# Loading queries and keys in long rows and turning them two tokens at a time: one change to an attention and MLP-mixer kernel on Trainium2

## The chip, the cores and the metric

The kernel runs on one core of one Trainium2 chip. A core has a matrix engine (PE, with its weight loads shown apart as PEld), a vector engine (DVE), a scalar engine (ACT), a third elementwise engine (POOL) and a sequencer that issues transfers (SP). Each runs its own list of instructions in order, and they wait for each other through semaphores. Data comes from the chip's main memory into the on-chip buffer by 16 DMA engines; a transfer is issued from the queue of SP or of ACT. PE writes its products into an accumulator memory of eight banks (`ps` in the code), from which DVE and ACT copy them out.

The metric is device time in microseconds (us): the median over runs of the whole program. Lower is better.

## The reference

Two blocks follow each other, all in 32-bit floats as far as the inputs go. The first is attention with routing: queries and keys are each assigned to one of 16 centroids per head, and a query sees only keys of its own cluster. The second is an MLP mixer over tokens, then over channels.

```python
batch, n_heads, seq, head_dim = (4, 8, 768, 64)      # 16 centroids per head
q_n, k_n, c_n = (each divided by its norm + 1e-06)
q_assign = np.argmax(np.einsum('bhsd,hcd->bhsc', q_n, c_n), axis=-1)
k_assign = np.argmax(np.einsum('bhsd,hcd->bhsc', k_n, c_n), axis=-1)
mask = q_assign[:, :, :, None] == k_assign[:, :, None, :]
scores = np.where(mask, 0.125 * np.matmul(q, k.transpose(0, 1, 3, 2)), -1000000000.0)
attn = softmax(scores)                               # over the keys
x = np.matmul(attn, v)                               # to (4, 768, 512), heads side by side
h = np.maximum(x.transpose(0, 2, 1) @ w_tok1, 0.0) @ w_tok2     # 768 -> 256 -> 768
u = x + h.transpose(0, 2, 1)
out = u + np.maximum(u @ w_ch1, 0.0) @ w_ch2         # 512 -> 1536 -> 512
```

The mixer's weights come as 64-bit floats and are rounded to 32 bits on the chip, in 31 pieces.

## The kernel before

**Pairs of heads.** The 32 heads of the four batches are worked on as 16 pairs, `pair(m)` for m = 0 to 15. For one pair, the scores need keys and queries with the 64 head dimensions of both heads on the 128 partitions, and the tokens along the line: the tile `Ts[m % 3]`, twelve blocks of 128 tokens, six of keys (rows 0 to 5) and six of queries (rows 6 to 11). The inputs lie the other way round, tokens first, so each block has to be transposed.

**Two ways to get there.** From pair 3 on, keys and queries are loaded into `qkr` in rows of 1536 bytes (six tokens of one head), split into 16-bit halves on ACT (`part_qk`, L1054), transposed by DMA, and joined again on ACT (`join_qk`, L1068). The first three pairs take a shorter way: `load_qk` (L915) loads them into `qks[m % 2]`, and `turn_qk` (L1036) transposes them on PE. In that buffer a partition holds six tokens, and for each token the 64 dimensions of head 0 next to those of head 1. To lay them out so, `load_qk` issues four transfers for a pair (keys and queries, each head by itself), in rows of 256 bytes (one token of one head). `turn_qk` takes the 128 values of a token position, both heads, as the input of one transpose (`turn`, L853); four transposes fill one bank of `ps`, and one copy (`copy`, L862) of 128 partitions x 512 moves the bank into `T`. That is twelve transposes and three copies a pair. In the profile all transposes and most matrix products have the line of `mm` (L846), copies on ACT have L865, copies on DVE L867, and transfers L905.

**The start.** `begin()` (L946) loads the centroids, then pair 0 on two queues (head 0 on SP, head 1 on ACT), then pair 1 and the first values on SP. While the loads are on their way PE multiplies the identity matrix by itself twelve times (`keep_busy(BUSY)`), and DVE normalises the centroids (`norm`, up to L997). Then pair 0 is turned, the centroids are turned between its banks and copied into `cbd` on DVE, and ACT loads its table for exponentials once `Ts[0]` is complete (L1007).

**Routing.** `route(m, bank)` (L1079) multiplies keys and queries with the centroids on PE, and DVE finds the largest of each group of 16: transpose (L1098), maximum, comparison, transpose back. For pair 0 the result is written straight into the mask operand `M0` in eight pieces (DVE L1131 and L1136, ACT L1129); for later pairs it goes through main memory (`wdm`). `scores(m)` (L1161) works in twelve chunks over three pairs of banks: two products of keys and queries, two products that add the mask, and one exponential on ACT (L1205) over both heads. For pair 0, three chunks' products are issued ahead, then pair 1 is turned, then the masks follow, and after the third mask the routing of pair 1, `route(1, 6)`. `values` (L1249) multiplies the exponentials with the values; pair 2 is turned between the third and the fourth of pair 0's six groups of value products, and routed after the sixth.

**The order of the work.** All operations are first collected in a `Program`, with the buffers that they read and write, and a cost for each engine that may do them. A planner (L152) then runs a list schedule: PE's operations stay in the order in which they were added, each other engine takes what it can start, the one with the earliest due time first. An operation that may run on ACT or DVE goes to the engine that would finish it first. An `after` gives the earliest planned time of an operation: `START + STEP * n` for the load of weight piece n. The planned order is what each engine's instruction list is written in.

**After the pairs**, DVE rounds what is left of the weight pieces (L1380 to L1390, L885), and the token and channel mixing runs on PE, with sums on DVE and POOL (L885).

## Time and profile before

| | |
|---|---|
| median of three runs | 789.43 us (789.10 to 789.65) |
| profiled execution | 789.87 us |
| its span | 788.0 us |
| PE busy | 777.8 us (99%) |
| DVE busy | 675.2 us (86%) |
| ACT busy | 461.4 us (59%) |
| POOL busy | 194.1 us (25%) |

The profile is one execution, recorded by the hardware. Times of its rows count from the start of the span; the 1.9 us that the execution takes beyond the span lie around it. Rows of the chain and of the timeline give a start, a length, an engine with the line of the code, and a count where several instructions are merged; a bracket tells how long the engine stood idle before and what ended that. Rows of waits give a sum, how often, and the longest. Rows of instruction groups give the shape, the count, the busy time and the mean in ns. Rows of windows give, for a stretch of time, its length, the busy time and instruction count of each engine in it, and at the end PE's granted clock, the busy share of the DMA engines and their GB/s. Rows of the DMA view give the size of a transfer and the time from issue to landing.

### The profile page before, as it was taken

The numbers are of one execution on the slowest core, as the hardware profiler recorded it, in microseconds if no ns is written. First come the engines' busy times: TensorE is split into PE (matmuls) and PEld (weight loads), VectorE is DVE, ScalarE is ACT, GpSimd is POOL, SyncE is SP. The second block draws the span as 40 slices with busy tenths as digits, with TensorE's granted clock in tenths as the row PEclk, the third lists the DMA queues.
The fourth block names the chain that finished last, engine by engine and source line by source line (L and its number), as shares of the span: only waits on it lengthen the run. The fifth ranks groups of instructions, "written<-read, shape, count | busy, mean of one in ns | idle before, by whom it ended". The sixth has DMA issues, their size and how long they took to land.

```text
span 788.0 us, 15324 instructions
## 1 busy us (share of the span) xinstructions
PE 777.8 (99%) x5975; PEld 463.1 (59%) x5975; DVE 675.2 (86%) x848; ACT 461.4 (59%) x614; POOL 194.1 (25%) x187
## 2 busy tenths in 40 slices
PE   8999999999999999999999999999999999999996
PEld 5666666666666666545555555555555555555554
DVE  6979999999998999999999877999853576799964
ACT  5788888889889875599614368633235204400422
POOL 0000000000000000001274598700285289830000
PEclk9999999999999999999999999999999999999999
DMA  9676668876778953568848999975788744444666
GB/s 249 169 192 180 170 154 221 212 202 178 196 196 215 266 178 128 127 135 202 195 124 253 313 281 266 273 189 132 168 189 177 165 100 101 105 105 102 160 164 161
DMA packets 326576, 143.68 MB, mean 182 GB/s; under 512 B 260192, under 2 KB 322400, under 8 KB 326496
## 3 DMA queue, kind: packets, MB, share of 16 engines
q1 hardware_dynamic: 324128, 141.83, 71.6%
q8 instruction: 49, 0.80, 0.4%
q10 hardware_dynamic: 2368, 0.79, 0.4%
q14 instruction: 31, 0.25, 0.1%
HBM read 91.95 MB, written 28.61 MB: 153 GB/s over the span
## 4 chain that ended last, share of the span: by engine, by line
PE 95%; DVE 3%; DMA 1%; issue 0%; ACT 0%; SPq 0%
PE ps L846 77%; PE ps L1238 18%; DVE arena L885 2%; DMA arena<-in_q_dram 1%; DMA arena<-in_moe_w_ch_dram 0%; ACT arena L865 0%; DVE arena L1384 0%; DVE arena L1390 0%; DVE arena L1387 0%; SPq L905 0%; DVE arena L1380 0%; DVE arena L867 0%; ACT arena L1129 0%
## 5 line engine op out<-in xcount | busy, mean ns | idle before, releaser
L846 PE MATMUL ps<-arena 128*128 128x384 f32 (+5 forms) x2727 | 640.2, 463 | 4.5 <-POOL arena masks.py:199 1.4
L846 PEld LDWEIGHTS ps<-arena 128*128 128x128 f32 (+2 forms) x2343 | 340.1, 184 | 250.3 <-issue 61.6
L885 DVE TENSOR_TENSOR arena<-arena 128x1536 f32<-128x1536 f32 (+6 forms) x340 | 369.9, 1109 | 12.5 <-issue 3.6
L885 POOL TENSOR_TENSOR arena<-arena 128x384 f32<-128x384 f32 x181 | 193.4, 1109 | 501.8 <-DVE arena L885 378.6
L885 DVE TENSOR_TENSOR arena<-ps,arena 128x384 f32<-128x384 f32 (+3 forms) x227 | 189.4, 844 | 78.4 <-PE ps L846 76.0
L875 ACT COPY arena<-arena 128x768 uint16<-128x768 uint16 x221 | 189.2, 955 | 62.6 <-DMA arena<-arena 32.8
L1205 ACT ACTIVATE arena<-ps 128x768 f32<-128x768 f32 x192 | 150.7, 811 | 35.2 <-PE ps L846 33.4
L1238 PE MATMUL ps<-arena 128*32 128x192 f32 (+1 forms) x3248 | 144.9, 335 | 0.0
L1238 PEld LDWEIGHTS ps<-arena 128*32 128x32 f32 x3248 | 103.7, 110 | 44.1 <-issue 15.6
L865 ACT COPY arena<-ps 128x512 f32<-128x512 f32 (+2 forms) x44 | 31.3, 719 | 116.1 <-PE ps L846 114.8
L892 ACT ACTIVATE arena<-arena 128x1152 f32<-128x1152 f32 (+1 forms) x38 | 39.7, 1070 | 51.0 <-DVE arena L885 50.3
L1912 ACT ACTIVATE arena<-arena 128x768 f32<-128x768 f32 x40 | 38.7, 969 | 32.8 <-DMA arena<-in_moe_w_ch_dram 27.1
L846 PEld LDWEIGHTS <-arena 64*128 64x128 bf16 x384 | 19.2, 94 | 24.6 <-issue 0.2
L1390 DVE SCALAR_TENSOR_TENSOR arena<-arena 128x512 f32<-128x512 uint32 (+1 forms) x31 | 21.5, 713 | 0.4
L1384 DVE SCALAR_TENSOR_TENSOR arena<-arena 128x512 uint32<-128x512 uint32 (+1 forms) x31 | 20.9, 695 | 0.3
L1108 ACT ACTIVATE arena<-arena 128x384 bf16<-128x384 f32 x16 | 11.2, 701 | 13.6 <-issue 13.6
L1380 DVE TENSOR_SCALAR arena<-arena 128x512 uint32<-128x512 uint32 (+1 forms) x31 | 13.9, 458 | 4.0 <-DMA arena<-in_moe_w_tok_dram 4.0
L1285 DVE STREAM_TRANSPOSE arena<-ps 128x768 f32<-128x768 f32 x16 | 15.2, 952 | 0.4 <-PE ps L1238 0.4
L1387 DVE TENSOR_SCALAR arena<-arena 128x512 uint32<-128x512 uint32 (+1 forms) x31 | 12.8, 436 | 0.4
L1293 DVE STREAM_TRANSPOSE arena<-ps 128x384 f32<-128x384 f32 x16 | 9.3, 579 | 2.2 <-PE ps L1238 2.0
L1098 DVE STREAM_TRANSPOSE arena<-ps 128x384 f32<-128x384 f32 x16 | 9.1, 571 | 1.8 <-PE ps L846 1.8
L1103 DVE STREAM_TRANSPOSE arena<-arena 128x384 f32<-128x384 f32 x16 | 9.3, 578 | 0.6
(57 smaller groups left out, 47.2 us busy)
## 6 DMA issues: line engine op xcount, KB each, us to landing
arena<-wd SPq DMA_DIRECT2D x196, 192.0 KB, 3.0
wd<-arena SPq DMA_DIRECT2D x84, 224.0 KB, 3.0
arena<-in_moe_w_ch_dram SPq DMA_DIRECT2D x96, 128.0 KB, 3.1
arena<-in_moe_w_ch_dram SPq DMA_DIRECT2D x16, 768.0 KB, 5.3
arena<-in_v_dram SPq DMA_DIRECT2D x16, 384.0 KB, 4.8
out_dram<-arena SPq DMA_DIRECT2D x14, 384.0 KB, 3.5
arena<-in_k_dram SPq DMA_DIRECT2D x13, 384.0 KB, 4.2
arena<-in_q_dram SPq DMA_DIRECT2D x13, 384.0 KB, 4.2
```

What stands on the lines that cost most here:

```text
L846: nc.tensor.matmul(dst, lhsT=lhsT, rhs=rhs, start=start, stop=stop, tile_position=pos, is_transpose=tr, skip_group_check=True,)
L865: nc.scalar.copy(out=dst, in_=src)
L875: nc.scalar.copy(out=dst, in_=src)
L885: (nc.vector if e == "DVE" else nc.gpsimd).tensor_tensor(out=dst, in0=a, in1=b, op=op)
L892: nc.scalar.activation(out=dst, in_=src, func=ACT.Relu)
L1205: lambda e, ex=ex, s=s, u=u: nc.scalar.activation(out=ex.ap[:, :, u * HS : (u + 1) * HS], in_=ps[:, 2 * s : 2 * s + 2, 0:HS], func=ACT.Exp ...
L1238: nc.tensor.matmul(dst, lhsT=lhsT, rhs=rhs, start=start, stop=stop, tile_position=pos, skip_group_check=True,)
L1285: lambda: nc.vector.transpose(out=x.ap[:, :, cols].rearrange("p j (c d) -> p c j d", d=32), in_=ps[:, 6:8, 0:HS],),
L1380: vec(lambda: nc.vector.tensor_scalar(out=hh, in0=hi, scalar1=0x07FFFFFF, scalar2=3, op0=ALU.bitwise_and, op1=ALU.logical_shift_left,), f, ...
L1384: vec(lambda: nc.vector.scalar_tensor_tensor(out=TT, in0=hi, scalar=0xC0000000, in1=hh, op0=ALU.bitwise_and, op1=ALU.bitwise_or), 0.14 + 0 ...
L1390: vec(lambda: nc.vector.scalar_tensor_tensor(out=ll, in0=lo, scalar=float(2.0**-52), in1=hh.bitcast(F32), op0=ALU.mult, op1=ALU.mult,), 0. ...
L1912: lambda e, i=i, func=func, bias=bias, n=n, hi=hi: nc.scalar.activation(out=hi, in_=hi, func=func, bias=bias, accum_out=wsum.ap[:, i, n : ...
```

## The change

For the first three pairs:

- `load_qk` issues two transfers a pair, one for the keys and one for the queries, each of both heads, in rows of 1536 bytes (six tokens of one head). The buffer `qks` now holds, on each partition, head 0's six tokens and then head 1's. For pair 0 the keys go on ACT's queue and the queries on SP's.
- `turn_qk` takes two neighbouring tokens of one head as the 128 values of a transpose. Three transposes fill 384 columns of a bank with one head's keys or queries; the even tokens come out on partitions 0 to 63, the odd ones on 64 to 127. Two copies, one for each half of the partitions, each 64 partitions x 384, bring them to the half of `T` that belongs to the head, into every second block. That is twelve transposes and eight copies a pair, over four banks.
- In `begin()` the centroids are turned after all of pair 0, not between its banks.
- In `scores(0)` the key half of pair 1 is turned ahead of the three score chunks, the query half after them.
- Pair 2 uses four banks in place of three.
- Of the planner's numbers: 9 warm-up products in place of 12, the weight pieces from time 7 on in place of 9, a shorter time to landing for the centroids and a shorter normalisation.

```diff
-BUSY, HITS_AT = 12, 18.0
+BUSY, HITS_AT = 9, 18.0
-START, STEP = 9, 10
+START, STEP = 7, 10
-    qks = [buf(3 + 6 * i, [2, NJ, 2, D]) for i in range(2)]
+    qks = [buf(3 + 6 * i, [2, 2, NJ, D]) for i in range(2)]
...
     def load_qk(m, after=0.0, queues=("SP", "SP")):
         b, hp = divmod(m, H // 2)
         t = qks[m % 2]
-        for i, a in ((1, k), (0, q)):
-            for h, qu in enumerate(queues):
-                dma(
-                    t.ap[:, i, :, h],
-                    a[b, 2 * hp + h].rearrange("(p j) d -> p j d", p=P),
-                    [], [("qk", m % 2, i, h)] + (t.rows(i, i + 1) if h else []), 192, 256,
-                    after, qu,
-                )
+        for (i, a), qu in zip(((1, k), (0, q)), queues):
+            dma(
+                t.ap[:, i].rearrange("p h j d -> p h (j d)"),
+                a[b, 2 * hp : 2 * hp + 2].rearrange("h (p j) d -> p h (j d)", p=P),
+                [], t.rows(i, i + 1), 384, 1536, after, qu,
+            )
...
-        dma(cen.ap[:, 0:D], centroids.rearrange("h c d -> (h c) d"), [], cen.k(), 32, 256)
-        load_qk(0, 0.0, ("SP", "ACT"))
+        dma(
+            cen.ap[:, 0:D], centroids.rearrange("h c d -> (h c) d"), [], cen.k(), 32, 256,
+            more=-1.7,
+        )
+        load_qk(0, 0.0, ("ACT", "SP"))
...
-        g.add({"DVE": 4.0}, norm, cen.k(), sq.k() + nsq.k())
-        turn_qk(0, (0, 1, 2), (0, 1))
+        g.add({"DVE": 3.0}, norm, cen.k(), sq.k() + nsq.k())
+        turn_qk(0, (0, 1, 2, 4))
         turn(ps[:, 7, 0:P], sq.ap[:, 0:P], sq.k(), bank(7))
-        turn_qk(0, (0, 1, 2), (2,))
...
-    def turn_qk(m, banks, parts=range(3)):
+    def turn_qk(m, banks, parts=range(4)):
+
         src, T = qks[m % 2], Ts[m % 3]
         for n in parts:
             bk = banks[n]
-            for i in range(4):
-                a, j = divmod(4 * n + i, NJ)
-                a = 1 - a
+            a, h = divmod(n, 2)
+            for i in range(HJ):
                 turn(
                     ps[:, bk, i * P : (i + 1) * P],
-                    src.ap[:, a, j].rearrange("p h d -> p (h d)"),
-                    [("qk", m % 2, a, 0), ("qk", m % 2, a, 1)] + src.rows(a, a + 1), bank(bk),
+                    src.ap[:, 1 - a, h, 2 * i : 2 * i + 2].rearrange("p j d -> p (j d)"),
+                    src.rows(1 - a, 2 - a), bank(bk),
                 )
-
-            copy(
-                T.ap[:, 4 * n : 4 * n + 4].rearrange("p a t -> p (a t)"), ps[:, bk], 512,
-                bank(bk), T.rows(4 * n, 4 * n + 4),
-            )
+            for j in range(2):
+                copy(
+                    T.ap[D * h : D * h + D, NJ * a + j : NJ * (a + 1) : 2],
+                    ps[D * j : D * j + D, bk, 0:HS].rearrange("p (i t) -> p i t", t=P), HS,
+                    bank(bk), sum((T.rows(NJ * a + i, NJ * a + i + 1) for i in range(j, NJ, 2)), []),
+                )
...
         ahead = 3 if m == 0 else 0
+        if m == 0:
+            turn_qk(1, (7, 6), (0, 1))
         for n in range(ahead):
             plain(n)
         if m == 0:
-            turn_qk(1, (7, 6, 7))
+            turn_qk(1, (0, 0, 7, 6), (2, 3))
             load_qkr(3, 18.0)
...
             if i == 3 and m == 0:
-                turn_qk(2, (1, 2, 3))
+                turn_qk(2, (1, 2, 3, 4))
```

5 lines of the change are left out of this document (3 added, 2 removed).

## The prediction

> **What bounds the kernel now.** I read the page first, for the engine that carries the span.
>
> ```profile
> span 788.0 us, 15324 instructions
> ...
> PE 777.8 (99%) x5975; PEld 463.1 (59%) x5975; DVE 675.2 (86%) x848; ACT 461.4 (59%) x614; POOL 194.1 (25%) x187
> ```
>
> PE, the matrix engine, works 777.8 of 788.0 us, and the change removes none of its work in the steady part. So only the time in which PE stands still is on offer. Second came the waits of PE alone, third the chain that ended last, in order of time.
>
> ```profile
> PE ps L846 <- POOL arena masks.py:199: 1.4, 1, 1.4
> PE ps L846 <- DVE arena L885: 1.3, 4, 0.5
> PE ps L846 <- ACT arena L865: 0.9, 2, 0.7
> PE ps L846 <- DMA arena<-in_q_dram: 0.7, 1, 0.7
> ```
>
> ```profile
> 1.93 5.20 DMA arena<-in_q_dram
> ...
> 7.26 0.42 PE ps L846 x2
> ...
> 7.71 1.14 ACT arena L865 x2
> ...
> 8.89 3.71 PE ps L846 x24
> ...
> 12.63 0.59 ACT arena L865
> 13.22 0.40 ACT arena L1129
> 13.62 0.96 ACT arena L865 x2
> ...
> 14.63 8.32 PE ps L846 x62
> ...
> 28.45 4.04 PE ps L1238 x96
> ...
> 408.61 1.36 DVE arena L885
> ...
> 410.02 371.11 PE ps L846 x1154
> ```
>
> The first group of lines is the start: the last query load lands at 1.93 + 5.20 = 7.13, the transposes and two ACT copies lead to pair 0's routing at 8.89, and pair 1's routing at 14.63 again waits for copies (L865). From 14.63 PE runs without a break worth the name until DVE (L885) holds it near 410; after 410.02 it runs to the tail. A start that is shorter by x therefore ends the kernel x earlier, unless the stretch before 410 takes it back.
>
> **The loads.** Four loads of 192 KB per pair, in rows of 256 bytes, become two of 384 KB in rows of 1536 bytes. The first fence has two issues from the timeline. The second has the times from issue to landing, by single windows of the DMA view. The third has the rates of two stretches in its last column, one with 256-byte rows in flight, one with 1536-byte rows:
>
> ```profile
> 0.74 0.65 ACTq L905 DMA_DIRECT2D arena<-in_k_dram  x1
> ...
> 1.19 0.69 SPq L905 DMA_DIRECT2D arena<-in_k_dram  x1
> ```
>
> ```profile
> arena<-in_k_dram ACTq DMA_DIRECT2D x1, 192.0 KB, 3.7
> ...
> arena<-in_q_dram SPq DMA_DIRECT2D x1, 192.0 KB, 5.2
> ...
> arena<-in_v_dram SPq DMA_DIRECT2D x1, 384.0 KB, 3.3
> ...
> arena<-in_v_dram SPq DMA_DIRECT2D x2, 384.0 KB, 4.5
> ```
>
> ```profile
> 6.00:7.00 1.00, 0.56 (x6) 0.32 (x3) 0.01 (x1) 0.59 (x1) 0.00 (x0) 1.00 1.35 218
> 10.00:11.00 1.00, 1.00 (x8) 0.76 (x6) 0.95 (x2) 0.35 (x2) 0.00 (x0) 1.00 1.05 376
> ```
>
> 384 KB (393 thousand bytes) take 1.80 us at 218 GB/s and 1.05 us at 376. A pair's 786 thousand bytes go from 3.6 to 2.1 us. The key load is now the first on ACT's queue (0.74), the query load the second on SP's (1.19 in place of 1.93). The value load that had the DMA engines nearly to itself took 3.3 us; behind a full queue the median was 4.5. So queries land between 1.19 + 3.3 = 4.5 and 1.19 + 4.5 = 5.7. I take 0.74 + 3.3 for the keys, one more transfer of 1.05 for the queries and 0.1 for the centroids: 5.2. That is 1.9 us before 7.13. The issues themselves (0.65 us each in the old form, four of them) get fewer; SP then reaches its later loads sooner, and nothing on the chain waits for those.
>
> [...]
>
> **Warm-up and transposes.** Three of the twelve warm-up products go. Each is two passes; the third line holds 24 passes and the first six key transposes.
>
> ```profile
> 1.36:4.60 3.24, 3.24 (x15) 3.24 (x16) 2.26 (x10) 1.49 (x2) 0.00 (x0) 1.00 0.76 173
> 4.80:5.60 0.80, 0.80 (x9) 0.80 (x9) 0.73 (x5) 0.00 (x0) 0.00 (x0) 1.00 1.34 236
> ```
>
> ```profile
> 1.36 5.20 PE L846 MATMUL ps<-arena 128*128 128x128 f32 x30 [1.36 <-POOL arena masks.py:199]
> ```
>
> 15 passes took 3.24 us, 0.21 each; nine later ones took 0.80, 0.09 to 0.11 each. PE is slow until about 4.7, though the clock column reads 1.00 in both rows. The six passes that go are fast ones, so warm-up ends 0.6 earlier, near 5.1, and the step has already turned by then. The transposes stay twelve a pair at 0.11: the key ones run 5.1 to 5.8, the query ones to 6.4, the centroids' one, now last, to 6.5. PE is then ahead of the copies.
>
> **The copies.** Three copies of 128x512 a pair become eight of 64 partitions x 384, so 9 become 24 in pairs 0 to 2.
>
> ```profile
> L865 ACT COPY arena<-ps 128x512 f32<-128x512 f32 x15 | 8.4, 585 | 12.4 <-PE ps L846 12.3
> L865 ACT COPY arena<-ps 128x384 f32<-128x384 f32 x15 | 7.2, 479 | 58.1 <-PE ps L846 56.9 <-DVE arena L885 1.2
> ...
> L867 DVE COPY arena<-ps 128x384 f32<-128x384 f32 x5 | 2.8, 550 | 0.2 <-PE ps L846 0.2
> ...
> L867 DVE COPY arena<-ps 64x64 f32<-64x64 f32 x2 | 0.4, 222 | 1.8 <-PE ps L846 1.8
> ```
>
> No row shows 64 partitions x 384. From below it is the 64x64 row, 0.22; from above 0.48 on ACT and 0.55 on DVE, the rows of the same length on all partitions. I take the upper ends, less 0.05 for the overlap of neighbours (two 512 copies at 13.62 took 0.96, not 1.17): what counts is elements in a line, not lines. So 1.76 us of copies a pair become about 3.8, now on two engines. DVE is free for them when the centroids are normalised:
>
> ```profile
> 5.12 0.42 DVE L997 TENSOR_SCALAR arena<-arena 128x64 f32<-128x64 f32 x2
> ...
> 8.86 1.28 ACT L1007 ACT_TABLE_LOAD   x1
> ```
>
> Pair 0: the first copy can start at 5.1 + 0.5 = 5.6. By the planner's rule (the engine that would finish first) I give ACT five of eight, 5.6 + 5 x 0.43 = 7.8, and DVE, from 6.0, three and the two centroid copies: 3 x 0.5 + 2 x 0.22 = 1.9, to 7.9. Routing starts near 7.9 against 8.89: 1.0 us saved, not 1.9, because copies are what comes last once the load is early. The table load (1.28) still follows the copies on ACT, which keeps pair 1's four key copies waiting until about 9.3; done by 11.1, they are ahead of PE's need.
>
> **From pair 0's routing to pair 1's.**
>
> ```profile
> 9.81 0.58 DVE L1098 STREAM_TRANSPOSE arena<-ps 128x384 f32<-128x384 f32 x1 [1.54 <-PE ps L846]
> ...
> 12.23 0.97 DVE L1131 TENSOR_SCALAR arena<-arena 32x384 bf16<-32x384 f32 x2
> ```
>
> Before, 14.63 - 8.89 = 5.74 us lie between the two; the chain's PE part ends at 8.89 + 3.71 = 12.6, the rest waits for copies of pair 1 behind one mask on ACT (L1129). The key half of pair 1 is now turned before the three score chunks, so its copies are covered by those. Only the query half, six transposes and four copies, stands at the end: PE reaches it at about 7.9 + 3.7 = 11.6 (the piece of 3.71 held routing, the score chunks and four transposes; now it holds six, without the drain of the last). Its copies are free to start at 12.2 and 12.5, and shared by two engines (2 x 0.5) they end near 13.2. DVE's masks begin at 7.9 + (12.23 - 8.89) = 11.2, so the first four are written before that. Pair 1's routing starts at 13.2 against 14.63: 1.4 us saved. If DVE stays with its masks and ACT does all four, it ends at 13.8 (0.8 saved).
>
> **Pair 2 and later.** Its eight copies come between two groups of value products, where ACT is idle and the next need for them, the routing of pair 2, lies 4.04 us of products later (28.45, L1238): nothing on the path. The cover is 4 us against 8 x 0.45 = 3.6 on ACT alone, so it just holds. Extra DVE work, some eight copies of 0.55, is 4.4 us. What can take it:
>
> ```profile
> 42.70 0.36 DVE L1380 TENSOR_SCALAR arena<-arena 128x384 uint32<-128x384 uint32 x1 [3.96 <-DMA arena<-in_moe_w_tok_dram]
> ...
> 14.60:297.00 282.40, 282.37 (x4051) 175.91 (x4055) 263.65 (x344) 239.39 (x319) 0.00 (x0) 1.00 0.75 198
> 297.00:383.00 86.00, 85.94 (x617) 45.68 (x610) 83.16 (x123) 65.80 (x86) 7.53 (x8) 1.00 0.61 146
> 383.00:410.10 27.10, 26.10 (x80) 14.36 (x78) 26.65 (x44) 8.01 (x8) 14.49 (x14) 1.00 0.70 178
> ```
>
> DVE idles 282.4 - 263.65 = 18.7 us before 297, 3.96 of it in one piece before 42.70. I cost it at nothing. The weight pieces, planned 2 us earlier (START), shift with PE; also nothing.
>
> **The sum.** Load -1.9, copies of pair 0 +0.9, the rest of the start -0.4: -1.4 us. The profiled execution took 789.87 (span 788.0 and 1.87 around it), 0.44 over the median of 789.43. 789.87 - 1.4 = 788.5; against the median 788.0.
>
> **Rivals.** *The whole load gain arrives.* If half-partition copies are nearer the lower end, or the planner's split is tighter, route 0 starts at 7.0 to 7.4 and the two short PE waits of this stretch (0.9 together) go as well: 1.9 to 2.5 saved, 787.2. For it: copies are all that stands between. Against it: each is as long in elements as a row that took 0.48.
>
> *Copies of one bank take turns.* If a copy on DVE starts only after ACT's copy of the other half of that bank, DVE's three follow one behind the other: 6.9, 7.5, 8.1, then the last at 8.7 with the centroid copies, and routing starts at 8.9, as now; pair 1's query copies end near 14.8. Time 789.5. No row shows two engines on one bank. [...]
>
> *DVE becomes late before 410 (slower).* In the 113 us from 297 to 410 DVE idles 3.3 us, and it is DVE that releases PE at 410.02. If the 4.4 us of copies, or a new order of the weight pieces, are not taken up before 297, they come out there, less the 1.4 saved: 792.4 at the worst, 791.3 if three quarters arrive. It decides once more than 1.4 us of DVE's delay reach that stretch. Against it stand the 18.7 us of idle time.
>
> **Numbers.** Forecast case 0.45 (788.0, itself 787.4 to 788.6), whole gain 0.24, turns 0.16, DVE late 0.15. Faster by over 0.2% means under 787.85, about what a measurement of this kernel can tell: the whole gain, and 0.17 of the forecast case, 0.41. Slower means over 791.0: 0.12 of the DVE case and 0.04 of the others, 0.16. The rest, 0.43, is within. The range runs from 786.9, below the whole gain, to 791.3, leaving out half of the DVE case and a little below.
>
> **What would show it.** The chain should show a query load of about 4.0 us from 1.19, ACT and DVE copies (L865, L867) from 5.6, routing near 7.9, and unbroken PE from about 13.2. Wrong would be: queries landing after 5.7; routing not before 8.5; a PE wait for DVE longer than 1.0 us between 383 and 410; or eight copies far shorter than 0.4 us.

## The result, and the profile after

| | before | changed |
|---|---|---|
| median, same chip | 789.65 us (5 runs) | 793.75 us (5 runs, 793.05 to 794.61) |
| ratio | | 1.0051, 95% interval 1.0038 to 1.0065 |
| profiled execution | 789.87 us | 793.05 us |
| its span | 788.0 us | 791.2 us |

The changed kernel is 4 us slower. The forecast was 788.0, and its range ended at 791.3. The recorded execution took 793.05, the lowest of the five times, against 789.87, so the two traces can explain 3.2 us of the 4.1 between the medians; what may be behind the rest comes further down.

The page of the changed kernel, first its span and engines:

```profile
span 791.2 us, 15316 instructions
...
PE 778.3 (98%) x5969; PEld 464.4 (59%) x5969; DVE 678.0 (86%) x853; ACT 466.1 (59%) x624; POOL 194.1 (25%) x187
```

PE works 778.3 us against 777.8: it has no more to do, it stands still for longer. The chain of the changed kernel, in order of time, says where:

```profile
0.74 0.44 SPq L905
...
1.24 4.34 DMA arena<-in_centroids_dram
...
6.30 0.20 ACT arena L986
6.50 0.36 ACT arena L865
6.87 0.48 ACT arena L865
7.36 0.47 ACT arena L865
7.84 0.48 ACT arena L865
...
8.85 0.56 DVE arena L867
...
10.03 4.29 PE ps L846 x29
...
14.41 0.56 DVE arena L867
...
14.99 0.48 ACT arena L865
...
15.49 0.48 ACT arena L865
...
16.00 0.57 DVE arena L867
...
16.61 1.69 PE ps L846 x11
```

Pair 0 is routed at 10.03 (before 8.89), pair 1 at 16.61 (before 14.63). The chain does not begin with a key or query load but with the centroids; behind them come their normalisation and then copies alone. The timeline of SP shows why the centroids come first in that chain:

```profile
0.74 0.44 SPq L905 DMA_DIRECT2D arena<-in_q_dram  x1
1.24 0.46 SPq L905 DMA_DIRECT2D arena<-in_centroids_dram  x1
```

and the DMA view of the first microsecond and a half gives the landings, in us from the issue:

```profile
arena<-in_k_dram ACTq DMA_DIRECT2D x1, 384.0 KB, 4.7
arena<-in_q_dram SPq DMA_DIRECT2D x1, 384.0 KB, 4.4
arena<-in_centroids_dram SPq DMA_DIRECT2D x1, 32.0 KB, 4.3
```

With the shorter landing time (`more=-1.7`) and the shorter normalisation, the planner found the centroids less urgent than the queries and issued them second. They landed at 5.58 and not at 2.58, and the normalisation ran from 5.60 to 8.43. One step of it is ACT's (L986, at 6.30) and stands ahead of the copies in ACT's list, so that ACT's first copy began at 6.41, though PE had written pair 0's first bank at 5.98; DVE's copies stand behind the whole of it. The keys, on ACT's queue, landed at 5.39, last of the two large loads. The waits of PE in the changed kernel:

```profile
PE ps L846 <- DVE arena L867: 2.5, 2, 1.3
PE ps L846 <- DVE arena L999: 1.5, 1, 1.5
```

The normalisation (L999) and DVE's copies (L867) together held PE for 4.0 us; neither was among PE's longer waits before. Further on, the products of pair 1's scores, in the chain of the changed kernel, end at 45.56:

```profile
34.47 11.09 PE ps L846 x74
45.56 6.67 PE ps L1242 x144
```

Before, that piece took 10.54 and ended at 43.02. PE shows no wait in it, because the two heads' products run side by side (before, they start 0.007 us apart) and one head's can hide that the other's stand still. In the changed kernel one head's product waited until 37.22 for a bank that held pair 2's routing, while the other head's went on, and the two stayed out of step. DVE had made three copies of pair 2 (before, ACT made all of that pair's) ahead of its weight roundings, and read that bank late:

```profile
30.98 1.73 DVE L867 COPY arena<-ps 64x384 f32<-64x384 f32 x3
...
36.63 0.54 DVE L1100 STREAM_TRANSPOSE arena<-ps 128x384 f32<-128x384 f32 x1
```

This transpose starts 2.2 us after the scores' piece; before, it started 1.0 us after it (33.46 against 32.48).

The ledger of the two traces, then: routing of pair 0 +1.14 us, from there to pair 1's routing +0.84, the scores of pair 1 +0.56, from there to PE's last product +0.51 (739.81 against 739.30). That is 3.05 us. The copies behind it, groups by shape:

```profile
L865 ACT COPY arena<-ps 64x384 f32<-64x384 f32 x18 | 8.4, 472 | 4.2 <-PE ps L846 2.9 <-DVE arena L867 1.1
...
L867 DVE COPY arena<-ps 64x384 f32<-64x384 f32 x6 | 3.3, 557 | 1.3 <-ACT arena L865 0.9 <-PE ps L846 0.2
```

A copy of 64 partitions is as long as one of 128 (472 against 479 ns on ACT, 557 against 550 on DVE), as the prediction took it. What it did not take is the split, eighteen on ACT and six on DVE, and that each engine waited for the other.

### The profile page after: what moved, and what is told of

Its sections match the earlier page's. It is cut to its first block, busy times and chain, and to the rows that moved or that the text cites. A ratio compares the mean times of both kernels' runs of the same rounds, so it can differ in the third digit from the quotient of the medians.

```text
span 791.2 us, 15316 instructions
## 1 busy us (share of the span) xinstructions
PE 778.3 (98%) x5969; PEld 464.4 (59%) x5969; DVE 678.0 (86%) x853; ACT 466.1 (59%) x624; POOL 194.1 (25%) x187
## 4 chain that ended last, share of the span: by engine, by line
PE 83%; DMA 7%; ACT 6%; DVE 2%; issue 0%; SPq 0%; ACTq 0%; DVEq 0%
PE ps L846 65%; PE ps L1242 18%; DMA arena<-in_moe_w_ch_dram 5%; ACT arena L1916 2%; ACT arena L875 2%; ACT arena L892 1%; DVE arena L885 1%; DMA arena<-arena 1%; DMA arena<-in_centroids_dram 1%; DMA arena<-wd 0%; ACT arena L865 0%; DVE arena L867 0%; SPq L905 0%; DVE arena L1394 0%; DVE arena L1388 0%
## 5 line engine op out<-in xcount | busy, mean ns | idle before, releaser
L865 ACT COPY arena<-ps 64x384 f32<-64x384 f32 (+3 forms) x53 | 34.7, 657 | 110.8 <-PE ps L846 109.4
L1916 ACT ACTIVATE arena<-arena 128x768 f32<-128x768 f32 x40 | 38.7, 970 | 34.1 <-DMA arena<-in_moe_w_ch_dram 27.9
L867 DVE COPY arena<-ps 64x384 f32<-64x384 f32 (+3 forms) x15 | 9.3, 617 | 2.7 <-PE ps L846 1.5
```

The costliest lines, as they stand in the source:

```text
L865: nc.scalar.copy(out=dst, in_=src)
L1916: lambda e, i=i, func=func, bias=bias, n=n, hi=hi: nc.scalar.activation(out=hi, in_=hi, func=func, bias=bias, accum_out=wsum.ap[:, i, n : ...
```

## The experiments

Each kernel was timed beside the kernel before on the same chip (whose median was 789.6 to 790.0 each time). The ratio is not the quotient of the two medians (for r9_chosen_split that would be 1.0021): an interval that holds 1 says that the comparison as a whole shows no change, even where the medians lie apart. The starts are those of the recorded execution, in us; the last column is the time from the end of pair 1's scores to PE's last product.

| kernel | median us | ratio, 95% interval | routing 0 | routing 1 | rest |
|---|---|---|---|---|---|
| before | 789.65 | | 8.89 | 14.63 | 739.30 |
| changed | 793.75 | 1.0051 [1.0038, 1.0065] | 10.03 | 16.61 | 739.81 |
| r1_cen_first | 794.18 | 1.0053 [1.0036, 1.0070] | 9.28 | 15.86 | 739.85 |
| r2_numbers_only | 794.29 | 1.0075 [1.0036, 1.0115] | 10.98 | 18.45 | 739.85 |
| r3_halves_only | 793.37 | 1.0049 [1.0032, 1.0066] | 10.04 | 17.55 | 739.85 |
| r4_rows_only | 789.48 | 1.0004 [0.9982, 1.0026] | 7.90 | 13.64 | 739.61 |
| r5_by_bank | 794.09 | 1.0045 [1.0026, 1.0065] | 8.76 | 17.11 | 739.88 |
| r6_by_parity | 794.42 | 1.0045 [1.0020, 1.0071] | 9.68 | 17.16 | 740.04 |
| r7_pair2_old_form | 793.85 | 1.0051 [1.0029, 1.0073] | 8.88 | 15.46 | 741.22 |
| r8_rows_9_products | 789.20 | 1.0003 [0.9976, 1.0029] | 7.29 | 13.02 | 739.25 |
| r9_chosen_split | 791.34 | 1.0011 [0.9995, 1.0028] | 9.23 | 15.91 | 739.84 |
| r10_half_width | 790.77 | 1.0013 [0.9989, 1.0038] | 10.23 | 15.96 | 739.84 |
| r11_old_numbers | 793.90 | 1.0058 [1.0032, 1.0084] | 9.66 | 17.21 | 739.29 |
| r12_pair0_only | 791.69 | 1.0024 [1.0014, 1.0033] | 8.81 | 14.54 | 741.22 |
| r13_pair0_start9 | 789.66 | 0.9991 [0.9972, 1.0011] | 8.40 | 14.13 | 740.50 |
| r14_split_start9 | 790.54 | 1.0009 [1.0000, 1.0018] | 9.20 | 15.57 | 739.08 |
| r15_start7_only | 790.06 | 1.0005 [0.9996, 1.0014] | 9.10 | 14.83 | 739.89 |

In r5_by_bank and r11_old_numbers the routing of pair 0 starts with some of its products; the rest follow at 9.82 and 10.64.

### One part at a time: the loads, the numbers, the copies

Two theories stood at the beginning: the late centroids (A), or the eight copies (B).

`r1_cen_first`, the changed kernel with the centroids issued first again:

```diff
-        dma(
-            cen.ap[:, 0:D], centroids.rearrange("h c d -> (h c) d"), [], cen.k(), 32, 256,
-            more=-1.7,
-        )
+        dma(cen.ap[:, 0:D], centroids.rearrange("h c d -> (h c) d"), [], cen.k(), 32, 256)
```

> The changed kernel with one thing undone: the planner's shorter landing time for the centroids (-1.7) is taken out, and with that SP issues the centroids first again, ahead of the queries. Theory A (the late centroids are the loss): they land near 2.6 in place of 5.58, the normalisation ends near 5.6, pair 0's routing starts at 8.3 to 8.6 in place of 10.03, and the time is about 791.5, half of the loss or more gone. Theory B (the copies are the loss): ACT still has seven copies of 0.48 one after the other behind the landing at 5.1 to 5.4, so routing starts near 9.4 at the earliest, and the time stays at 792.5 to 793.5.

Measured 794.18, above what either theory forecast. The centroids landed at 2.89, and both routings came 0.75 us earlier in the trace than in the changed kernel, but the medians (794.18 and 793.75) do not show it, and routing of pair 0 still starts 0.39 after the kernel before. The timelines of ACT and of DVE in r1_cen_first, the last bracket giving the wait:

```profile
5.82 3.40 ACT L865 COPY arena<-ps 64x384 f32<-64x384 f32 x7 [2.00 <-PE ps L846]
```

```profile
7.31 1.03 DVE L867 COPY arena<-ps 64x384 f32<-64x384 f32 x3 [1.56 <-ACT arena L865]
```

DVE had been done with the normalisation since 5.75 and made one copy of pair 0 (the row's other two are the centroids', 64x64); ACT made seven. In the planner's own times DVE is taken by the normalisation when the first copies come up, and that is decided before the kernel runs. Theory A alone falls.

`r2_numbers_only`, the kernel before with the four numbers alone:

```diff
-BUSY, HITS_AT = 12, 18.0
+BUSY, HITS_AT = 9, 18.0
-START, STEP = 9, 10
+START, STEP = 7, 10
...
+            more=-1.7,
...
-        g.add({"DVE": 4.0}, norm, cen.k(), sq.k() + nsq.k())
+        g.add({"DVE": 3.0}, norm, cen.k(), sq.k() + nsq.k())
```

> The kernel before with nothing but the planner's four numbers of the change (9 warm-up products, weight pieces from 7, centroids' landing -1.7, normalisation 3.0). SP then issues one key load ahead of the centroids. Theory A: the centroids land about 1 us later than 2.58, which the queries' landing at 7.13 still covers, so routing stays within 0.3 of 8.89 and the time within 0.5 of before; if the numbers themselves were the loss, it would be 791 or more. Theory B: no change from before, 789.6.

Measured 794.29, 4.3 us slower than before: my expectation was wrong. The centroids' load, issued behind a key load, landed at 6.07; their transpose, and with it the four query transposes behind it on PE, waited until 8.98. The timeline of PE in r2_numbers_only:

```profile
7.02 0.41 PE L846 MATMUL ps<-arena 128*128 128x128 f32 x2 [1.12 <-DMA arena<-in_q_dram]
8.98 1.33 PE L846 MATMUL ps<-arena 128*128 128x128 f32 x5 [1.55 <-DVE arena L1001]
```

And PE then lost its clock. Windows of r2_numbers_only, PE's clock in the column after the five engines:

```profile
8.90:10.40 1.50, 1.33 (x5) 0.93 (x5) 0.90 (x6) 0.06 (x1) 0.00 (x0) 0.50 1.19 275
11.00:15.00 4.00, 4.00 (x16) 1.71 (x18) 2.30 (x5) 1.43 (x2) 0.00 (x0) 0.51 1.16 310
```

The same four microseconds' worth in the kernel before:

```profile
8.90:12.90 4.00, 4.00 (x28) 2.45 (x28) 2.91 (x6) 1.72 (x3) 0.00 (x0) 1.00 1.14 300
```

16 passes instead of 28 in 4 us, at a clock of 0.51: routing and the score chunks of pair 0 took 5.46 instead of 3.71 us. So 1.75 us of this kernel's loss is a second slow phase, behind two gaps of 1.12 and 1.55 us.

`r3_halves_only`, the kernel before with each copy in two halves of the partitions:

```diff
-            copy(
-                T.ap[:, 4 * n : 4 * n + 4].rearrange("p a t -> p (a t)"), ps[:, bk], 512,
...
+            for j in range(2):
+                hs = slice(D * j, D * j + D)
+                copy(
+                    T.ap[hs, 4 * n : 4 * n + 4].rearrange("p a t -> p (a t)"), ps[hs, bk], 512,
```

> The kernel before with each copy of 128x512 made into two of 64 partitions x 512, so 18 copies in place of 9; loads, transposes and numbers as before. Theory A: the start moves little, routing by 0.5 or less, time 789.6 to 790.2. Theory B: a copy of half the partitions takes as long as one of all (0.58), and a copy on DVE out of a bank waits until ACT's copy out of it is done; routing of pair 0 about 0.6 to 0.9 later than 8.89, that of pair 1 1.5 or more later than 14.63, time 791 or more.

Measured 793.37. Nothing but twice as many copies, and 3.4 us are gone. The queries landed at 7.04 (before 7.13), and still routing started at 10.04 and 17.55. Groups by shape of r3_halves_only:

```profile
L865 ACT COPY arena<-ps 64x512 f32<-64x512 f32 x14 | 7.7, 580 | 8.4 <-PE ps L846 8.3
...
L867 DVE COPY arena<-ps 64x512 f32<-64x512 f32 x4 | 2.7, 687 | 2.8 <-ACT arena L865 2.7
```

`r4_rows_only`, the other half: the long rows with the transposes and copies as they were. It measures the loads alone: the first three pairs get tokens and heads in other places than the reference wants, with as much work.

```diff
-                    src.ap[:, a, j].rearrange("p h d -> p (h d)"),
+                    src.ap[:, a].rearrange("p h j d -> p (h j d)")[:, P * j : P * j + P],
```

> The kernel before with the loads of the change alone: rows of 1536 bytes, two loads a pair, keys on ACT's queue, centroids first. Transposes, copies and numbers stay as before, so the first three pairs are fed with tokens and heads in the wrong places and their results are not the reference's; the amount of work is the same. Both theories: queries land near 5.4 in place of 7.13, routing of pair 0 starts at 7.2 to 7.4, and 1.5 us reach the end: 788.0. If the load was not what held the start, 789.6.

Measured 789.48, routing at 7.90 and 13.64: 1.0 us earlier than before, but later than the 7.2 to 7.4 expected, and the interval holds no change. Here twelve warm-up products still held the transposes, so `r8_rows_9_products`, which feeds the pairs in the same wrong places, took nine (`BUSY, HITS_AT = 9, 18.0`):

> r4_rows_only (the kernel before with the long-row loads alone; transposes and copies are as before, so the tokens and heads of the first three pairs land in other places than the reference wants, with as much work) with 9 warm-up products instead of 12. In r4_rows_only PE's transposes began at 5.65 because the warm-up held them, with the keys there about 1.5 us earlier. Theory full load gain: transposes begin at 5.1, routing of pair 0 at 7.3 to 7.5 (before 8.89, r4_rows_only 7.90), pair 1 at 13.1; all 0.5 us earlier than in r4_rows_only, time 789.0 against 789.95, 1.5 us under the kernel before in the trace. Rival (queries land last): the second bank waits for the queries, which land near 5.4, and routing stays at 7.8 to 7.9.

Routing at 7.29 and 13.02, 1.6 us before the kernel before, as expected; the median, 789.20, is only 0.5 us lower, and the interval holds no change. The load gain is real in the trace (the recorded execution took 787.92), it is not shown in the medians, and it is the whole of what this change had to offer. The DMA view of r8_rows_9_products gives the landings from the issues at 0.74 and 1.19:

```profile
arena<-in_k_dram ACTq DMA_DIRECT2D x1, 384.0 KB, 3.2
arena<-in_q_dram SPq DMA_DIRECT2D x1, 384.0 KB, 3.8
```

### Whose turn is it: two engines and one bank

In the changed kernel a copy by one engine waits, by a semaphore, for the copy of the other half of the same bank by the other engine (the chain from 14.41 to 16.57: DVE, ACT, ACT, DVE). `r5_by_bank` ties each bank to one engine, `r6_by_parity` makes the engines share every bank; both have the centroids first.

```diff
                     bank(bk), sum((T.rows(NJ * a + i, NJ * a + i + 1) for i in range(j, NJ, 2)), []),
+                    (("ACT",), ("DVE",))[h],
```

(`[j]` in place of `[h]` in r6_by_parity.)

> The changed kernel with the centroids issued first again (as in r1_cen_first) and with its half-partition copies tied to an engine by bank: the banks of head 0 are emptied by ACT alone, those of head 1 by DVE alone. As many copies as in r1_cen_first, of the same length, only no bank is shared by two engines. Theory turns (two copies of one bank on two engines follow one another, and this is what stretches the last four copies of pair 1 to 2.2 us in r1_cen_first): the four query copies of pair 1 become two beside two, 1.0 to 1.2 us instead of 2.2; routing of pair 1 starts 0.9 to 1.3 us earlier than in r1_cen_first (15.86), at 14.6 to 15.0; pair 0's at 8.7 to 9.1 (9.28); the time is about 793.0. Rival length (the number of copies and their length alone decide, and the planner's split was no worse than another): routing of pair 1 within 0.4 us of 15.86, time 794.

> As r5_by_bank, but the other way round: of every bank, ACT copies partitions 0 to 63 and DVE partitions 64 to 127, so that every bank is shared. The engines have the same four copies each a pair as in r5_by_bank. Theory turns: in each bank DVE starts only when ACT has ended, so that the last bank's DVE copy starts one ACT copy late; the four query copies of pair 1 take 0.48 + 0.56 + 0.56 = 1.6 us or more instead of r5_by_bank's 1.1, and routing of pair 1 starts 0.4 to 0.7 us later than there, at 15.2 to 15.6. In the trace no two copies of one bank overlap. Rival (two engines read different halves of a bank at once, and the order seen before had other reasons): copies of one bank overlap, and routing of pair 1 starts within 0.2 us of r5_by_bank's.

Measured 794.09 and 794.42; routing of pair 1 at 17.11 and 17.16, both later than 15.86. The waits are where the theory has them. DVE's copies in r5_by_bank wait for PE alone:

```profile
7.01 2.75 DVE L867 COPY arena<-ps 64x384 f32<-64x384 f32 x6 [1.32 <-PE ps L846]
```

and in r6_by_parity for ACT:

```profile
7.45 2.55 DVE L867 COPY arena<-ps 64x384 f32<-64x384 f32 x6 [1.91 <-ACT arena L865]
```

The bank is what the copies take turns over, not the place that they write: in r3_halves_only two copies of one bank write different partitions of `T`, and DVE waits for ACT all the same (2.7 us); in r5_by_bank both engines write the same blocks of `T` on different partitions, out of different banks, and copies of the two run at the same time (ACT from 7.00, DVE from 7.01).

But taking the turns away gained nothing, and the two kernels do not differ in what counts. In r5_by_bank DVE had been free since 5.70 and began when PE had written the last bank (6.98), because that bank's copy stood first in its list; and pair 1's key copies (12.50 to 13.62) stood in DVE's list in the middle of pair 0's routing, between the comparison and the transpose back, so that the masks came 1.1 us later. The turns exist; the order of DVE's list decides.

### Where the copies are placed, and which pairs have them

`r7_pair2_old_form` is r1_cen_first with the third pair loaded, turned and copied as before:

```diff
+        if m == 2:
+            for n in range(3):
...
+                copy(
+                    T.ap[:, 4 * n : 4 * n + 4].rearrange("p a t -> p (a t)"), ps[:, bk], 512,
```

> r1_cen_first with pair 2 in its old form: four loads in rows of 256 bytes, twelve transposes of both heads, three copies of 128x512. Pairs 0 and 1 as in r1_cen_first. In that kernel and in the changed one the scores of pair 1 take 0.55 us more of PE's time than before (11.09 from 33.72 to 44.81, before 10.54). Theory pair 2 (its eight copies, which the prediction costed at nothing, hold ACT and DVE when the exponentials and the transpose of pair 2's routing are due): the stretch is 10.5 again, and all that follows is 0.5 to 0.6 us earlier, the time 793.6. Rival (the stretch is longer because of pair 1's own late start): it stays at 11.1 and the time at 794.2.

The stretch of pair 1's scores is what it was before, from the chain of r7_pair2_old_form:

```profile
33.32 10.54 PE ps L846 x80
43.85 6.66 PE ps L1269 x144
```

So the 0.55 us there come from pair 2's new form; DVE has one copy of pair 2 here, not three, and reads the routing's bank earlier. The median, 793.85, does not fall, since this kernel lost 1.4 us later (741.22 against 739.85).

`r9_chosen_split` places the copies of pairs 0 and 1 by hand on top of that:

```diff
+A, V = ("ACT",), ("DVE",)
+SPLIT = [[(A, A), (V, V), (A, A), (A, A)], [(A, A), (A, A), (A, A), (V, V)]]
...
+                    SPLIT[m][n][j], EARLY[n][j] if m == 0 else 0.0,
```

> r7_pair2_old_form with the copies of pairs 0 and 1 placed by hand: pair 0's second bank (keys of head 1) on DVE, due before everything else there, the other six copies on ACT; of pair 1 the keys and head 0's queries on ACT, head 1's queries on DVE. No bank of a pair is shared, DVE copies what is ready first, and the routing chain of pair 0 on DVE has no copy in its midst (as it had in r5_by_bank). This is nearly the split that the prediction assumed for pair 0 (five and three). Theory placement (the copies cost as much as they do because the planner puts seven of eight on ACT): DVE's two copies and the centroids' two end near 7.9, ACT's six 0.49 apart from 5.4 to 5.8 on end at 8.4 to 8.7; routing of pair 0 at 8.4 to 8.75 (r7 8.88, before 8.89), pair 1's at 14.0 to 14.5 (r7 15.46, before 14.63), PE's end 1.0 to 1.4 us before r7's, time 792.5 or below. Rival (eight copies of that length are simply too many, wherever they go): routing of pair 1 not before 15.0, time as r7_pair2_old_form, 793.9.

Measured 791.34, 2.5 us under r7_pair2_old_form, though the recorded execution routes pair 1 at 15.91, later than the 14.0 to 14.5 expected. `r12_pair0_only` takes the old form for pair 1 too (`if m:` in place of `if m == 2:`):

> r9_chosen_split with pair 1 in its old form too (four loads in rows of 256 bytes, twelve transposes of both heads after the score chunks, three copies of 128x512); only pair 0 has the long rows, the two-token transposes and the eight copies, placed as in r9_chosen_split. Theory pair 1 (what r9_chosen_split still loses, 791.34 against 789.69, lies between the two routings: PE stood 1.31 us behind pair 1's query copies, before 0.24): from pair 0's routing to pair 1's it is 5.7 us again (r9 6.68), pair 1's routing 5.7 after a start at 8.4 to 9.2, at 14.1 to 14.9, time 789.3 to 790.3. Rival (the start of pair 0 carries it, with PE slow for as long as in r9_chosen_split, until 6.6): routing of pair 1 later than 14.9 and the time 791. In neither case a gain over the kernel before that 0.2% would show.

Routing at 8.81 and 14.54, with 5.73 between the two, as the theory had it; but the median was 791.69, and the 2.0 us were lost behind pair 1's scores (741.22 against 739.30). Waits of PE in r12_pair0_only between 380 and 430:

```profile
PE ps L851 <- DVE arena L890: 1.4, 4, 0.5
...
PE ps L851 <- issue: 0.6, 1, 0.6
```

### What the planner's START does far from the start

This is where the weight pieces are rounded. START is the number that plans them 2 us earlier. `r13_pair0_start9` and `r14_split_start9` set it back in r12_pair0_only and r9_chosen_split, `r15_start7_only` changes it alone in the kernel before:

```diff
-START, STEP = 9, 10
+START, STEP = 7, 10
```

> r12_pair0_only with the weight pieces planned from 9 on, as in the kernel before, instead of 7. In r12_pair0_only pair 1's routing started at 14.54 (before 14.63), the scores of pair 1 ended 0.09 us earlier than before, and all of its 2.0 us were lost later: 0.75 us by 411, 0.8 at 427, the rest behind that. Theory START (the number that moves the weight pieces 2 us earlier re-orders loads and roundings so that they come late from 383 on): the stretch from the end of pair 1's scores to PE's end is 739.3 to 739.9 us instead of 741.2, and the time is 789.3 to 790.3. Rival (any change of the start re-orders them, whatever this number is): the stretch stays at 740.5 to 741.5 and the time above 791.

> r9_chosen_split with the weight pieces planned from 9 on. Its stretch from the end of pair 1's scores to PE's end was 739.84 us against 739.30 before. Theory START: 739.3, time 0.5 us under r9_chosen_split's 791.34, at 790.8. Rival: no change.

> The kernel before with the weight pieces planned from 7 on instead of 9, and nothing else: the one number of the change that acts on the weights. The prediction costed it at nothing. Theory START: the stretch from the end of pair 1's scores (43.02 before) to PE's end is 0.5 to 2 us longer than 739.30, the time 790.2 to 791.7 against 789.7; the start as before. Rival: time within 0.3 us of the kernel before.

r15_start7_only: 790.06 against 789.72, an interval that holds no change, with the last stretch 0.59 us longer in the trace, as theory START had it, and the time just under the 790.2 that it gave. Its waits of PE between 380 and 430:

```profile
PE ps L846 <- DVE arena L885: 1.4, 4, 0.5
```

and those of the kernel before in the same window:

```profile
PE ps L846 <- DVE arena L885: 1.0, 3, 0.5
```

With START back at 9, r12_pair0_only's 791.69 became 789.66 and r9_chosen_split's 791.34 became 790.54: 2.0 and 0.8 us by the medians, 0.7 and 0.8 by the last stretch of the traces. So the number is not "nothing" in these two; alone, in r15_start7_only, it is not told from nothing by the medians. Nor is it the only thing: r3_halves_only has START 9 and the longer stretch all the same. A new order at the start can make the planner write another list for the weight pieces 400 us later; between 739.1 and 741.2 us came out of it.

In the changed kernel the 0.51 us of the last stretch does not lie here. From the end of pair 1's scores to 412.56 it takes 367.0 us, as before; the rest is one break of PE, at 517, in the chain of the changed kernel:

```profile
509.49 6.82 DMA arena<-in_moe_w_ch_dram
...
516.33 1.01 ACT arena L1916 x2
517.34 0.38 ACT arena L865
...
517.76 266.42 PE ps L846 x830
```

The copy that PE needed (L865) stood in ACT's list behind two operations on a weight piece (L1916) that landed at 516.31. r13_pair0_start9 lost 1.2 us at 515 in the same way, and its START is 9, so no run shows that START caused this break.

r13_pair0_start9, with the new form for pair 0 only and its copies placed by hand, is the best that this change gave: 789.66 against 789.72, no difference.

### The numbers undone, and full-width copies from long rows

`r11_old_numbers` is the changed kernel with all four numbers as before.

> The changed kernel with all planner numbers as before (12 warm-up products, weight pieces from time 9, no shorter landing of the centroids, normalisation 4.0): the new loads, transposes and copies alone. Theory two causes (the layout costs what r1_cen_first still lost, the numbers the rest): the centroids are issued first, the first copy comes 0.5 us later than in r1_cen_first because of the three more products, routing of pair 0 at 9.3 to 9.9, pair 1's at 15.9 to 16.5, PE's end at 784.6 to 785.2, time 794. Rival (the numbers are most of the loss, as r2_numbers_only suggests): routing of pair 0 at or under 8.9, time within 1 us of the kernel before.

793.90, as the changed kernel: in the new layout the four numbers together neither cost nor gave anything that the time shows. By the traces pair 1 is routed 0.6 us earlier in the changed kernel than here, with three warm-up products fewer and the centroids late, and the last stretch is 0.5 us longer. The layout carries the loss.

`r10_half_width` keeps copies of all 128 partitions with long rows, for pair 0, by a product with the identity for each head:

```diff
+                if m == 0:
+                    for h in range(2):
+                        mm(
+                            ps[D * h : D * h + D, bk, i * P : (i + 1) * P], long[:, a, h, j],
+                            ident.ap, True, True, 0.22,
...
+                            bank(bk), pos=(0, D * h),
+                        )
+                    continue
```

> The kernel before with pair 0 alone loaded in two transfers of long rows (keys on ACT's queue) and 9 warm-up products, but with full-width copies: each token's 64 values of one head are turned by a product with the identity matrix, head 0 into partitions 0 to 63 of the bank, head 1 into 64 to 127, so that three copies of 128x512 do as before. 24 products of 64 columns replace 12 transposes in pair 0; all other pairs as before. Theory copies (what spoils the long rows is only the eight copies): two products of neighbouring column halves run side by side, 0.22 us for the two, 2.6 us for pair 0 from 5.1 on; the last copy ends near 8.4 and routing starts at 8.3 to 8.5, 0.4 to 0.6 before 8.89; pair 1's at 14.0 to 14.2; time 789.2 against 789.7. Rival (the products run one after another, 0.22 each): 5.3 us, routing of pair 0 at 11, time 791.8.

790.77 against 789.69, an interval that holds no change, and neither of the two numbers. The products of the two heads overlapped: windows of the kernel before hold 8 full-width passes in 1.30 us while PE is slow (2.00:3.30) and 13 in 1.10 us later (4.90:6.00), those of r10_half_width 13 and 17. But in the first of these PE was still slow. Windows of PE in r10_half_width, early and late in this piece:

```profile
5.50:6.80 1.30, 1.30 (x13) 1.00 1.28 247
8.45:9.55 1.10, 1.10 (x17) 1.00 1.05 376
```

13 half-width passes in 1.30 us first, 17 in 1.10 later. Pair 0 took 4.0 us and not 2.6.

## Why the prediction was wrong

The terms can be told apart by the traces; in brackets are the two kernels and the stretch:

| term | us |
|---|---|
| the loads and nine warm-up products (before, r8_rows_9_products, routing of pair 1) | -1.61 |
| the two-token turns and eight copies of pairs 0 and 1 (r8_rows_9_products, r7_pair2_old_form, routing of pair 1) | +2.44 |
| centroids behind the queries (r7_pair2_old_form, changed, routing of pair 1) | +1.15 |
| the new form of pair 2 (r7_pair2_old_form, r1_cen_first, scores of pair 1) | +0.56 |
| a late weight piece, one break of PE at 517 (before, changed, last stretch) | +0.51 |
| sum | +3.05 |

The centroids' order is read against r7_pair2_old_form, not r1_cen_first, which runs the same code up to there but for the loads of pair 2. In r1_cen_first's recorded execution PE stayed slow for longer, its transposes began at 5.29 (r7_pair2_old_form 4.90), and the routings came 0.40 later; against it the term is 0.75. In the changed kernel no transpose fell into PE's slow phase: they began at 5.44, behind it, because the keys landed at 5.39. The medians of the three kernels (793.85, 794.18, 793.75) show nothing of this term, so it rests on the traces alone.

By the steps of the prediction:

- **The loads.** The queries landed at 5.09 where 5.2 was forecast. The keys came at 5.39 and not at 4.0. In the changed kernel's trace keys and queries were both issued at 0.74, on two queues, and took 4.7 and 4.4 us: neither finished well ahead of the other. But that was not the order that the prediction had assumed. In the twelve kernels that issue the centroids first and the queries 0.45 us behind the keys, the keys took 3.1 to 3.5 us and landed at 3.8 to 4.2, as forecast, about a microsecond or more ahead of the queries. The load term, 1.9, was close: r8_rows_9_products, with whole copies, has 1.6 us of it at both routings. The step that failed is "0.1 for the centroids": I added their transfer to the queries' and left them first in the queue. The prediction counted `more=-1.7` and the shorter normalisation nowhere, and with them the planner put the queries first; the centroids and the keys both came late. In the new layout this cost 1.15 us by the traces.
- **Warm-up and transposes.** The transposes began at 5.44, 0.3 late, because of the keys. That "the step has already turned by then" holds in this execution and not in all (below).
- **The copies.** The length of one was right, the 0.05 taken off for overlap was not: seven on ACT took 3.40 us in r1_cen_first, 0.49 each. The split was the larger error: "I give ACT five of eight" by the planner's rule, but the planner gave it seven, for by its plan DVE was still normalising; in the changed kernel it really was, until 8.43. "DVE is free for them when the centroids are normalised" names the condition itself, and the condition had moved by 3 us. Routing at 10.03 against 7.9 is the largest miss. With the centroids first and the copies placed by hand it is 8.40 at best (r13_pair0_start9), still 1.1 after r8_rows_9_products: that much more eight copies cost than three, in the best placement that was tried.
- **From pair 0's routing to pair 1's.** 6.58 us and not 5.3. "Shared by two engines (2 x 0.5)" was the error: four copies took 2.2 us one after another (14.41 to 16.57). r9_chosen_split, with each bank on one engine, came to 6.68, since DVE's two then wait behind its masks. PE stood 1.0 us or more here in every kernel with the new form of pair 1, and 0.24 in those with the old form and whole copies.
- **Pair 2 and later.** "Costed at nothing" was 0.56 us. The cover was named (4 us against 3.6, "it just holds"), and that it was that thin should have given the step a price; it looked at ACT, and it was with DVE's copies that the routing's bank came late. "The weight pieces, planned 2 us earlier, shift with PE; also nothing" was 0.51 us here and 1.9 in r12_pair0_only, of which setting START back took away 0.7.
- **The rivals.** *Copies of one bank take turns* had the mechanism: in the chain of the changed kernel the second engine starts when the first has ended (DVE to 14.97, ACT from 14.99; ACT to 15.97, DVE from 16.00). Its chance, 0.16, was the author's estimate. Its time, 789.5, lacked the rest, and r5_by_bank shows that the turns alone do not decide. Since the program itself puts a semaphore between the two copies, no run shows whether the bank would have let both read at once. *DVE becomes late before 410* did not come true in the changed kernel (367.0 us from the scores of pair 1 to 412.56, as before). The case that came, slower from the start itself, had no rival: every case had the load gain in it and asked only how much of it would stay.

What the traces do not settle is the difference between the medians and the recorded executions. It lies between 1.6 us over (r1_cen_first) and 0.9 us under (r10_half_width, r13_pair0_start9), and the changed kernel's own median is 0.7 over. The moment at which PE's clock steps up (below) may be a part of it: r9_chosen_split and r10_half_width were recorded with a late step and lie over their medians, r7_pair2_old_form and r8_rows_9_products with an early one and lie 1.3 under theirs. r13_pair0_start9, early and over, does not fit, unless its wait of 1.2 us near 515 was a single case. A second slow phase, as r2_numbers_only recorded it, may occur in other executions too. The mean clock that is on record for each execution speaks for it: in the changed kernel 793.05 and 793.07 us came with 0.999 and 1.000, the three longer times with 0.995 to 0.998; in r7_pair2_old_form five executions at 0.998 or 0.999 took 792.55 to 793.25, the seven at 0.995 to 0.997 took 793.36 to 798.58; all twelve of r9_chosen_split lie at 0.998 or 0.999 and within 790.69 to 791.97. A mean lower by 0.002 over 790 us stands for about 1.6 us at full clock lost (an estimate, 0.002 x 790). This may be why r9_chosen_split's median is 2.5 us under r7_pair2_old_form's, which the two recorded starts do not show. It is not proven: r11_old_numbers spreads from 792.12 to 795.00 at 0.997 to 0.999, and no trace was taken of such an execution. What PE waited for near 427 in r7_pair2_old_form and r12_pair0_only is open too.

## What to carry to other kernels

Where a planner orders the work, an edit of its numbers is an edit of the order: read from it what comes first in each queue and which engine each new operation goes to before pricing anything, and expect other lists in stages far from the edit (0.8 and 2.0 us by the medians of two pairs of kernels here). Price a copy by its elements in a line, and ask of each split copy where in its engine's list it will stand; a copy that needs half the partitions was no cheaper here (472 against 479 ns on ACT, 557 against 550 on DVE), and splitting three copies a pair into six cost more (3.4 us) than shorter loads gave (1.6 us by the trace). When an engine is to be "free from then on", write down what frees it and check that the change leaves that event where it was.

## What the hardware showed that was not expected

**PE's first slow phase had no fixed length.** r9_chosen_split, r12_pair0_only and r13_pair0_start9 run the same instructions for pair 0; each was recorded once. Windows of PE between 4.90 and 6.40, passes in parentheses, first of r9_chosen_split:

```profile
4.90:6.40 1.50, 1.50 (x9) 1.00 0.72 220
```

then of r12_pair0_only:

```profile
4.90:6.40 1.50, 1.50 (x14) 1.00 1.21 253
```

The first copies on ACT, in r9_chosen_split:

```profile
6.24 2.93 ACT L870 COPY arena<-ps 64x384 f32<-64x384 f32 x6 [2.58 <-PE ps L851]
```

in r12_pair0_only:

```profile
5.86 2.90 ACT L870 COPY arena<-ps 64x384 f32<-64x384 f32 x6 [2.27 <-PE ps L851]
```

and in r13_pair0_start9:

```profile
5.45 2.90 ACT L870 COPY arena<-ps 64x384 f32<-64x384 f32 x6 [1.87 <-PE ps L851]
```

Routing of pair 0 followed at 9.23, 8.81 and 8.40. The last pass at 0.21 us began at 6.42, 4.93 and 4.07. Over all traces it began 2.7 to 5.5 us after PE's first pass at 1.36. The clock column says 1.00 throughout, but the trace's record of the granted clock has its first entry only at the step (6.80, 5.30 and 4.44 in these three, 4.99 in the changed kernel, 4.74 in the kernel before): for the slow phase nothing is on record, and the column shows that as 1.00. The kernel before hides this: its queries land at 7.13, behind the last of these passes, whereas the changed kernel's transposes start at 5.4, in the middle of where the step falls. What sets the moment of the step, which moved over 2.8 us in these traces, no run shows.

**The clock went again in one run.** In r2_numbers_only it fell to 0.50 at 8.07, in the second of two gaps of 1.12 and 1.55 us with 0.41 us of work between them, and stayed there until 14.90. PE had worked 1.61 of the 3.30 us from 4.70 to 8.00. That the gaps made the clock fall was not shown.

**The small load was late behind a large one.** The centroids, 32 KB, landed 2.0 us after their issue as first in SP's queue (r4_rows_only, r8_rows_9_products), and 4.3 us after it as second, behind 384 KB (the changed kernel).
